# Cosine attention and token/channel mixing on one core: split score tiles, norms on ScalarE, permuted w2, squares further ahead

## Chip, cores and metric

The kernel runs on one core of one Trainium2 chip. The metric is device time in microseconds (us), median of several executions. The granted clock is the share of full speed that the profile shows. Kernels are compared only within the same rounds. The engines are PE (TensorE matmul), PEld (its weight load), DVE (VectorE), ACT (ScalarE), POOL (GpSimd) and SP (it issues most transfers). SBUF is the on-chip memory that holds the kernel's tiles, PSUM the one that its matmuls write to; copying a result from PSUM to SBUF is called its eviction.

## The reference

Cut to what matters:

```python
# q, k, v: (8, 12, 448, 64)
q_n = q / (norm(q, axis=-1) + 1e-6);  k_n = k / (norm(k, axis=-1) + 1e-6)
attn = softmax(q_n @ k_n.T / 0.1)
x = (attn @ v) -> (8, 448, 768)                        # heads side by side
u = x + (relu(x.T @ w_tok1) @ w_tok2).T                # token mixing, hidden size 256
out = u + relu(u @ w_ch1) @ w_ch2                      # channel mixing, hidden size 1536
```

## The kernel before

The work is 48 pairs of heads, six to a batch item. One loop iteration `i` does the scores of pair `i`, attn·v of pair `i-1` and the token step of about pair `i-2`; it also prepares later pairs (squares, sums, norms, scaling, transposes). Channel mixing of a batch item (`ch_units`) starts when its six pairs are done, so it cannot start before iteration 8, and from then on it is spread over the iterations by `feed`. A sequence position is split as `(p c)`, with `c` of size 4: row `4p+c` of the sequence sits in partition `p`, chunk `c`.

```python
    def squares(i, on_act=False):              # POOL, except in the prologue
        sq = nrm.tile([SC, 2, 2 * NCH, E], FP32, tag="sq", bufs=2)
        ...
                nc.gpsimd.tensor_mul(out=sq[:, a], in0=src, in1=src)
    def sums(i): nc.vector.tensor_reduce(out=ssq..., in_=sq, op=ALU.add)
    def rnorms(n, p0=0, p1=HP):                # 1/(sqrt(ssq) + eps)
        nc.scalar.activation(out=rn, in_=ssq, func=AF.Ln, bias=tiny[:])
        nc.scalar.activation(out=rn, in_=rn, func=AF.Exp, scale=0.5)
        nc.vector.tensor_scalar_add(out=rn, in0=rn, scalar1=EPS_NORM)
        nc.vector.reciprocal(out=rn, in_=rn)
    def scaled(i, dve=""): ...                 # qn, kn = q*rn, k*rn: POOL, or DVE where named

    def score(i, cg):                          # two chunks into one 4-bank PSUM tile, one exp
        psS = ps2.tile([128, 2, 2, 512], FP32, tag="s")          # ps2 has bufs=1
        ...
        nc.scalar.activation(out=st["pt"][:, cg], in_=psS[0:SC, :, :, 0:S], func=AF.Exp, scale=inv_tau)

    def m_tok2(i):                             # u = x + r @ w2, x added by four identity matmuls
        psU = ps.tile([128, S], FP32, tag="b")
        for tt in range(TT):
            nc.tensor.matmul(psU[:], st["r"][:, tt, :], w2t[:, tt, 0:S], start=(tt == 0), stop=False)
        for c in range(NCH):
            nc.tensor.matmul(psU[:].rearrange("d (p c) -> d c p", c=NCH)[:, c, :], st["x"][:, c, :],
                             id16[:, LEAD[c]:LEAD[c] + SC], start=False, stop=(c == NCH - 1))
        nc.vector.tensor_copy(out=ut[:, dt, 0:S], in_=psU[:])    # odd batch items: 384 and 64 columns
    ... # cut
    sq_at = at({p: p - 3 if p < 10 else max(p - 6, 2 + p // 2) for p in range(3, NP_ALL)})
    sc_at = at({p: p - 2 if p < DMA_FROM else p - 3 for p in range(2, NP_ALL)})
        # in iteration i, first: scaled(p) for p in sc_at[i], then squares(p) for p in sq_at[i]
        # at its end: sums(p), and for p < 15 rnorm1(p) at once
```

## Time and profile before

| | kernel before |
|---|---|
| time | 456.50 us median (456.25 to 456.67, 4 runs) |
| span of the profiled run | 455.0 us |
| busy | PE 408.4 (90%), DVE 202.8, ACT 236.8, POOL 213.5 us |

Shares over the whole span hide that there are two regimes. The table of busy time by stretch shows it. Its columns are the stretch and its length, then busy us and number of instructions of each engine, the granted clock, the DMA share and GB/s:

```profile
core 0: us, PE busy (x) PEld busy (x) DVE busy (x) ACT busy (x) POOL busy (x), PEclk, DMA share, GB/s
...
70.00:80.00 10.00, 1.89 (x15) 0.83 (x13) 8.55 (x7) 2.94 (x5) 9.98 (x11) 0.69 0.82 124
...
160.00:200.00 40.00, 39.77 (x414) 24.29 (x413) 19.71 (x49) 23.14 (x26) 25.82 (x25) 1.00 0.78 170
```

From 160 to 200 us PE is busy 99% of the time, so only PE work that disappears shortens that part. From 70 to 80 us PE does almost nothing and POOL is busy all the time. The clock column seems to miss a slow clock at the start: a group of four score matmuls takes 0.93 us at 56.89 us, where the column reads 0.50 (57 to 58 us), and 0.93 us at 21.28 us too, where it reads 1.00; later it takes 0.55 us.

In the PE-bound part, the chain of waits (start us, length us, what) gives the exact cost of each piece of PE work:

```profile
182.35 0.38 PE psU_2556 L257 x4
182.73 1.14 PE psG_0_2565 L269 x6
...
190.31 0.38 PE psU_2679 L257 x4
190.69 1.14 PE psG_4_2688 L269 x6
```

One iteration takes 190.69 - 182.73 = 7.96 us. The four identity matmuls of the token step (L257) take 0.38 us of it, 95 ns each.

In the early part the same chain goes round several engines:

```profile
60.94 1.14 DVE ssq_381 L155
62.10 0.32 ACT rn_382 L162
62.44 0.22 ACT rn_382 L163
62.69 0.18 DVE rn_382 L164
62.89 0.25 DVE rn_382 L165
...
64.29 1.04 POOL kn_817 L176
65.33 2.00 POOL sq_819 L150 x2
67.36 1.23 DVE ssq_381 L155
```

From one sum (L155) to the next is 67.36 - 60.94 = 6.42 us, and that is the length of an early iteration: the sum must wait for the squares, the squares stand behind the scaling in POOL's queue, and the scaling waits for the norm of the previous sum.

The standstill at 70 us, in the timeline (start, length, engine, line, operation):

```profile
70.14 1.48 POOL L135 CAST vt_95<-vs_380 112x1536 f16<-112x1536 f32 x1
...
71.36 6.27 DVE L164 TENSOR_SCALAR rn_382<-rn_382 112x16 f32<-112x16 f32 x1 [0.62 <-ACT rn_382 L163]
...
76.57 1.03 POOL L150 TENSOR_TENSOR sq_931<-kh_702 112x512 f32<-112x512 f32 x1
77.55 0.88 POOL L112 DMA_DIRECT2D wc2t<-in_moe_w_ch_dram  x1
...
78.56 0.53 PE L188 MATMUL pst_990<-id_83,kn_817 112*128 112x112 f16 x4 [8.11 <-DVE x_950 L225]
```

An add of 16 columns that takes 0.175 us elsewhere lasts 6.27 us while POOL runs one operation after another, and PE waits 8.11 us for DVE.

### The profile page before, as it was taken

The page shows a single profiled execution, that of the slowest core. Times are in us where ns is not written, and L with a number is a line of the kernel's source. Part 1 is how long each engine was busy: PE and PEld are TensorE (multiplying, and loading weights), DVE is VectorE, ACT ScalarE, POOL GpSimd, SP SyncE. Part 2 cuts the span into 40 slices and gives each one's busy share as a digit, 9 for nine tenths or more (in the row PEclk, how much of TensorE's full clock was granted, in tenths as well). Part 3 has the DMA queues.
Part 4 walks back from the last instruction along what each step waited for, and adds up shares of the span by engine and source line. Part 5 has one row for each costly group of instructions (what it writes and reads, how often), then busy time and mean ns, then how long its engine had stood idle before and what let it go on. Part 6 is the DMA issues. An engine that isn't in the chain of part 4 may idle for free.

```text
span 455.0 us, 9700 instructions
## 1 busy us (share of the span) xinstructions
PE 408.4 (90%) x4104; PEld 250.4 (55%) x4104; DVE 202.8 (45%) x458; ACT 236.8 (52%) x277; POOL 213.5 (47%) x216
## 2 busy tenths in 40 slices
PE   1377572899999999999999999999999999999995
PEld 0146451466655666556655666556656665566563
DVE  3656758565444354444534445446343433232000
ACT  3466543475466545675466455665565447630410
POOL 2686779391919265563838091926474330000000
PEclk9999987899999999999999999999999999999998
DMA  8999877752775169662685279733852233001012
GB/s 212 250 254 239 145 182 109 141 134 71 176 177 154 27 179 159 168 161 68 167 177 143 61 134 218 193 86 98 195 83 77 58 110 56 1 1 71 35 51 89
DMA packets 76411, 58.11 MB, mean 128 GB/s; under 512 B 36976, under 2 KB 72784, under 8 KB 76368
## 3 DMA queue, kind: packets, MB, share of 16 engines
q1 hardware_dynamic: 72704, 52.32, 48.0%
q0 software_dynamic: 3664, 5.18, 6.9%
q8 instruction: 32, 0.52, 0.5%
q14 instruction: 11, 0.09, 0.1%
HBM read 43.38 MB, written 11.01 MB: 120 GB/s over the span
## 4 chain that ended last, share of the span: by engine, by line
PE 80%; DVE 7%; ACT 6%; POOL 4%; issue 2%; DMA 1%; SPq 0%; ACTq 0%; POOLq 0%
DVE rn_382 L164 1%; DVE ssq_130 L155 1%; DVE ssq_381 L155 1%; DMA kh_104<-in_k_dram 1%; ACT pt_308 L210 1%; DVE ssq_118 L155 1%; DVE ssq_704 L155 0%; PE psG_2_1016 L269 0%; PE psF_1_0_3760 L288 0%; PE psF_1_0_2231 L288 0%; PE psF_0_0_2105 L288 0%; PE psF_2_1_1719 L288 0%; PE psF_1_0_5275 L288 0%; PE psF_1_1_1595 L288 0%; PE psF_0_1_1466 L288 0%
## 5 line engine op out<-in xcount | busy, mean ns | idle before, releaser
L269 PEld LDWEIGHTS <-wc1t 128*128 128x128 f16 x576 | 53.8, 101 | 45.1 <-issue 7.2
L233 PEld LDWEIGHTS <-w1t 128*128 128x128 f16 x384 | 22.7, 98 | 0.0
L288 PEld LDWEIGHTS <-gt_0_449 128*128 128x128 f16 x168 | 15.7, 98 | 10.9 <-issue 1.9
L288 PEld LDWEIGHTS <-gt_3_4834 128*128 128x128 f16 x168 | 15.9, 98 | 9.3
L288 PEld LDWEIGHTS <-gt_1_1784 128*128 128x128 f16 x168 | 15.8, 98 | 9.4 <-issue 0.4
L288 PEld LDWEIGHTS <-gt_2_3305 128*128 128x128 f16 x168 | 15.7, 98 | 9.5 <-issue 0.4
L188 PE MATMUL pst_156<-id_83,kn_154 112*128 112x112 f16 x4 | 0.6, 294 | 9.0 <-DVE kn_154 L176 9.0
L294 DVE COPY ost_0_6217<-psF_0_0_6218 128x384 f32<-128x384 f32 x1 | 0.6, 559 | 17.3 <-PE psF_0_0_6218 L291 17.3
L188 PE MATMUL pst_990<-id_83,kn_817 112*128 112x112 f16 x4 | 0.5, 286 | 8.1 <-DVE x_950 L225 8.1
L164 DVE TENSOR_SCALAR rn_382<-rn_382 112x16 f32<-112x16 f32 x3 | 6.6, 2206 | 1.9 <-ACT rn_382 L163 1.9
L176 POOL TENSOR_TENSOR qn_5263<-qh_4628,rn_4632 112x512 f16<-112x512 f32 x1 | 1.0, 1043 | 13.5 <-DVE rn_4632 L165 13.5
L176 POOL TENSOR_TENSOR qn_3745<-qh_3099,rn_3103 112x512 f16<-112x512 f32 x1 | 1.0, 1042 | 13.5 <-DVE rn_3103 L165 13.5
L176 POOL TENSOR_TENSOR qn_2216<-qh_1570,rn_1574 112x512 f16<-112x512 f32 x1 | 1.0, 1043 | 12.4 <-DVE rn_1574 L165 12.4
L176 POOL TENSOR_TENSOR qn_4510<-qh_3880,rn_3884 112x512 f16<-112x512 f32 x1 | 1.0, 1042 | 12.4 <-DVE rec_0_4542 L224 12.4
L176 POOL TENSOR_TENSOR qn_2981<-qh_2351,rn_2355 112x512 f16<-112x512 f32 x1 | 1.0, 1042 | 11.3 <-DVE rec_0_3013 L224 11.3
L176 POOL TENSOR_TENSOR qn_2611<-qh_1952,rn_1956 112x512 f16<-112x512 f32 x1 | 1.0, 1042 | 11.1 <-DVE rn_1956 L165 11.1
L176 POOL TENSOR_TENSOR qn_1839<-qh_1193,rn_1197 112x512 f16<-112x512 f32 x1 | 1.0, 1042 | 10.5 <-DVE rn_1197 L165 10.5
L176 POOL TENSOR_TENSOR qn_1452<-qh_808,rn_812 112x512 f16<-112x512 f32 x1 | 1.0, 1042 | 10.1 <-PE psO_0_1485 L221 10.1
L162 ACT ACTIVATE rn_107<-ssq_106,tiny 112x16 f32<-112x16 f32 x3 | 0.9, 307 | 9.1 <-DVE ssq_106 L155 9.1
L176 POOL TENSOR_TENSOR qn_4132<-qh_3481,rn_3485 112x512 f16<-112x512 f32 x1 | 1.0, 1044 | 9.6 <-DVE rn_3485 L165 9.6
L188 PEld LDWEIGHTS <-kn_154 112*128 112x128 f16 x4 | 0.3, 130 | 9.0 <-DVE kn_154 L176 9.0
L176 POOL TENSOR_TENSOR qn_4889<-qh_4246,rn_4250 112x512 f16<-112x512 f32 x1 | 1.0, 1042 | 9.0 <-DVE rn_4250 L165 9.0
(1681 smaller groups left out, 1266.8 us busy)
## 6 DMA issues: line engine op xcount, KB each, us to landing
wc1t<-in_moe_w_ch_dram POOLq DMA_DIRECT2D x2, 1152.0 KB, 10.9
wc2t<-in_moe_w_ch_dram POOLq DMA_DIRECT2D x2, 1152.0 KB, 9.5
qh_103<-in_q_dram SPq DMA_DIRECT2D x3, 224.0 KB, 4.3
kh_104<-in_k_dram SPq DMA_DIRECT2D x3, 224.0 KB, 4.6
vs_105<-in_v_dram SPq DMA_DIRECT2D x1, 672.0 KB, 7.0
qh_115<-in_q_dram SPq DMA_DIRECT2D x3, 224.0 KB, 8.1
kh_116<-in_k_dram SPq DMA_DIRECT2D x3, 224.0 KB, 8.3
vs_117<-in_v_dram SPq DMA_DIRECT2D x1, 672.0 KB, 10.7
```

The lines of the kernel that those rows point to most:

```text
L155: nc.vector.tensor_reduce(out=half[i // HP]["ssq"][:, :, lo:lo + 2 * NCH], in_=pipe[i]["sq"][:], axis=AXX.X, op=ALU.add)
L162: nc.scalar.activation(out=rn, in_=ssq, func=AF.Ln, bias=tiny[:])
L164: nc.vector.tensor_scalar_add(out=rn, in0=rn, scalar1=EPS_NORM)
L176: eng.tensor_tensor(out=dst[:].rearrange("p c g e -> p g c e"), in0=src, in1=_bcast_free(rn, E), op=ALU.mult)
L188: nc.tensor.transpose(pst[:, a, c, :], src[:, c], id16[:SC, :SC])
L210: nc.scalar.activation(out=st["pt"][:, cg], in_=psS[0:SC, :, :, 0:S], func=AF.Exp, scale=inv_tau)
L233: nc.tensor.matmul(psR[:, tt, :], w1t[:, m, tt * 128:(tt + 1) * 128], st["x"][:, m, :], start=(m == 0), stop=(m == NCH - 1))
L269: nc.tensor.matmul(psG[:], wc1t[:, dt, ct * 128:(ct + 1) * 128], ut[:, dt, span(b)], start=(dt == 0), stop=(dt == DT - 1))
L288: nc.tensor.matmul(psF[:], rows(gt, ct), wc2t[:, ct, dh * DH:(dh + 1) * DH], start=(ct == 0), stop=False)
L294: nc.vector.tensor_copy(out=o[:, 0:DH], in_=psF[:])
```

## The change

The intent: (1) take the add and the reciprocal of the norms from DVE, as two more ACT operations; (2) compute squares four pairs ahead (in the prologue and up to pair 11), with the norm one iteration after the sum, so that the loop over engines opens; (3) put the scores of one chunk in a 2-bank tile, two such tiles, one exp each; (4) place w2 in the order `(c p)` on chip, so that the identity matmuls write PSUM contiguously and the eviction undoes the order. Cut to its core:

```diff
-    ps2 = ctx.enter_context(tc.tile_pool(name="ps2", bufs=1, space=bass.MemoryType.PSUM))
+    ps2 = ctx.enter_context(tc.tile_pool(name="ps2", bufs=2, space=bass.MemoryType.PSUM))
+    def place_w2():
+        for tt in range(TT):
+            nc.gpsimd.tensor_copy(out=w2t[:, tt], in_=w2n[:, tt].rearrange("t (p c) -> t c p", c=NCH))
-        nc.vector.tensor_scalar_add(out=rn, in0=rn, scalar1=EPS_NORM)
-        nc.vector.reciprocal(out=rn, in_=rn)
+        nc.scalar.activation(out=rn, in_=rn, func=AF.Ln, bias=eps[:])
+        nc.scalar.activation(out=rn, in_=rn, func=AF.Exp, scale=-1.0)
-        psS = ps2.tile([128, 2, 2, 512], FP32, name=f"psS_{i}_{cg}", tag="s")
+        for c in range(c0, c1):
+            psS = ps2.tile([128, 2, 512], FP32, name=f"psS_{i}_{c}", tag="s")
+            ... # two matmuls
+            nc.scalar.activation(out=st["pt"][:, c], in_=psS[0:SC, :, 0:S], func=AF.Exp, scale=inv_tau)
-            nc.tensor.matmul(psU[:].rearrange("d (p c) -> d c p", c=NCH)[:, c, :], st["x"][:, c, :],
-                             id16[:, LEAD[c]:LEAD[c] + SC], start=False, stop=(c == NCH - 1))
+            nc.tensor.matmul(psU[:, c, :], st["x"][:, c, :], id16[:, LEAD[c]:LEAD[c] + SC],
+                             start=False, stop=(c == NCH - 1))
+        def rows(lo, n, p0, p1):
+            nc.vector.tensor_copy(out=ut[:, dt, lo:lo + n].rearrange("d (p c) -> d c p", c=NCH),
+                                  in_=psU[:, :, p0:p1])
-    sq_at = at({p: p - 3 if p < 10 else max(p - 6, 2 + p // 2) for p in range(3, NP_ALL)})
+    sq_at = at({p: p - 4 if p < 12 else max(p - 6, (p + 2) // 2) for p in range(4, NP_ALL)})
+    rn_at = at({p: p - 3 if p < 12 else (p + 4) // 2 for p in range(3, 15)})
-                scaled(p, dve="k" if p < 4 else "")
+            scaled(p, dve="k" if p < 7 else "")
-            if i == 0:
-                weights_tok()
+        if i == 1:
+            weights_tok()
+        if i == 2:
+            place_w2()
... # cut: order of loads and of the prologue, EARLY = 8 (below it, scores chunk by chunk)
```

More of the change, by code (lines that the diff above doesn't have):

```diff
@@ L81 @@
     nc.gpsimd.memset(tiny[:], 1e-18)
+    eps = cst.tile([SC, 1], FP32, name="eps")
+    nc.gpsimd.memset(eps[:], EPS_NORM)
     w1t = cst.tile([128, NCH, T], FP16, name="w1t")
-    w2t = cst.tile([128, TT, S + 384], FP16, name="w2t")
+    w2n = cst.tile([128, TT, S], FP16, name="w2n")
+    w2t = cst.tile([128, TT, NCH, SC], FP16, name="w2t")
     wc1t = cst.tile([128, DT, C], FP16, name="wc1t")
@@ L103, in weights_tok @@
         nc.gpsimd.dma_start(out=w1t[128 - SC:128, 3, :], in_=w1r[:, 3, :])
-        nc.gpsimd.dma_start(out=w2t[:, :, 0:S], in_=moe_w_tok2.rearrange("(tt p) s -> p tt s", p=128))
+        nc.gpsimd.dma_start(out=w2n[:], in_=moe_w_tok2.rearrange("(tt p) s -> p tt s", p=128))
+    def place_w2():
+        for tt in range(TT):
+            nc.gpsimd.tensor_copy(out=w2t[:, tt], in_=w2n[:, tt].rearrange("t (p c) -> t c p", c=NCH))
     def weights_ch1(i):
@@ L140, in sides, with squares @@
         return hf["q"][:, j:j + 2], hf["k"][:, j:j + 2]
-    def squares(i, on_act=False):
-        st = pipe[i] = {}
-        sq = nrm.tile([SC, 2, 2 * NCH, E], FP32, name=f"sq_{i}", tag="sq", bufs=2)
+    def squares(i, on_act=""):
+        if i not in pipe:
+            pipe[i] = {"sq": nrm.tile([SC, 2, 2 * NCH, E], FP32, name=f"sq_{i}", tag="sq", bufs=2)}
+        sq = pipe[i]["sq"]
         for a, src in enumerate(sides(i)):
             src = src.rearrange("p g c e -> p (g c) e")
-            if on_act:
+            if not on_act:
+                nc.gpsimd.tensor_mul(out=sq[:, a], in0=src, in1=src)
+            elif "qk"[a] in on_act:
                 nc.scalar.activation(out=sq[:, a], in_=src, func=AF.Square)
-            else:
-                nc.gpsimd.tensor_mul(out=sq[:, a], in0=src, in1=src)
-        st["sq"] = sq
     def sums(i):
@@ L188, in tpose, with qk_copy @@
                 nc.tensor.transpose(pst[:, a, c, :], src[:, c], id16[:SC, :SC])
-        nc.vector.tensor_copy(out=qk_tile(i)[:], in_=pst[:])
+        st["pst"] = pst
+    def qk_copy(i):
+        nc.vector.tensor_copy(out=qk_tile(i)[:], in_=pipe[i]["pst"][:])
     def dma_tpose(i):
@@ L195, in dma_tpose, with score @@
             nc.sync.dma_start_transpose(out=qk[:, a], in_=src[:].rearrange("p c g e -> p (c g e)"))
-    def score(i, cg):
+    def score(i, c0, c1):
         st = pipe[i]
         qk = st["qk"][:].rearrange("p a c s -> p (a c s)")
-        if cg == 0:
-            st["pt"] = ptp.tile([SC, 2, 2, 2, S], FP16, name=f"pt_{i}", tag="pt")
-        psS = ps2.tile([128, 2, 2, 512], FP32, name=f"psS_{i}_{cg}", tag="s")
-        for j in range(2):
-            c = 2 * cg + j
+        if c0 == 0:
+            st["pt"] = ptp.tile([SC, NCH, 2, S], FP16, name=f"pt_{i}", tag="pt")
+        for c in range(c0, c1):
+            psS = ps2.tile([128, 2, 512], FP32, name=f"psS_{i}_{c}", tag="s")
             for hh in range(2):
                 hb = hh * 64
-                nc.tensor.matmul(psS[:, hh, j, 0:S], qk[hb:hb + 64, c * SC:c * SC + 128],
+                nc.tensor.matmul(psS[:, hh, 0:S], qk[hb:hb + 64, c * SC:c * SC + 128],
                                  qk[hb:hb + 64, S:2 * S], start=True, stop=True)
-        nc.scalar.activation(out=st["pt"][:, cg], in_=psS[0:SC, :, :, 0:S], func=AF.Exp, scale=inv_tau)
+            nc.scalar.activation(out=st["pt"][:, c], in_=psS[0:SC, :, 0:S], func=AF.Exp, scale=inv_tau)
     def pv(i, hh):
@@ L220, in pv @@
             for c in range(NCH):
-                nc.tensor.matmul(psO[:, m, 0:E + 1], st["pt"][:, c // 2, hh, c % 2, lo:lo + 128],
+                nc.tensor.matmul(psO[:, m, 0:E + 1], st["pt"][:, c, hh, lo:lo + 128],
                                  vt[:, g, c, 0:E + 1], start=(c == 0), stop=(c == NCH - 1))
@@ L251, in m_tok2 @@
         ut = pairt[b // 2][0]
-        psU = ps.tile([128, S], FP32, name=f"psU_{i}", tag="b")
+        psU = ps.tile([128, NCH, SC], FP32, name=f"psU_{i}", tag="b")
         for tt in range(TT):
-            nc.tensor.matmul(psU[:], st["r"][:, tt, :], w2t[:, tt, 0:S],
-                             start=(tt == 0), stop=False)
+            nc.tensor.matmul(psU[:], st["r"][:, tt, :], w2t[:, tt], start=(tt == 0), stop=False)
         for c in range(NCH):
-            nc.tensor.matmul(psU[:].rearrange("d (p c) -> d c p", c=NCH)[:, c, :], st["x"][:, c, :],
-                             id16[:, LEAD[c]:LEAD[c] + SC], start=False, stop=(c == NCH - 1))
+            nc.tensor.matmul(psU[:, c, :], st["x"][:, c, :], id16[:, LEAD[c]:LEAD[c] + SC],
[3 more added lines that the diff above has]
+                                  in_=psU[:, :, p0:p1])
         if b % 2 == 0:
-            nc.vector.tensor_copy(out=ut[:, dt, 0:S], in_=psU[:])
+            rows(0, S, 0, SC)
         else:
-            nc.vector.tensor_copy(out=ut[:, dt, S + 64:2 * S], in_=psU[:, 0:384])
-            nc.vector.tensor_copy(out=ut[:, dt, S:S + 64], in_=psU[:, 384:S])
+            rows(S + 64, 384, 0, 96)
+            rows(S, 64, 96, SC)
     def m_ch1(b, ct):
@@ L330, in at, with gpsimd_part @@
         return got
-    load_at = at({p: p - 6 if p < 13 else max(p - 8, (p - 1) // 2) for p in range(9, NP_ALL)})
-    sq_at = at({p: p - 3 if p < 10 else max(p - 6, 2 + p // 2) for p in range(3, NP_ALL)})
+    load_at = at({p: p - 6 if p < 13 else max(p - 8, 6) for p in range(9, NP_ALL)})
+    sq_at = at({p: p - 4 if p < 12 else max(p - 6, (p + 2) // 2) for p in range(4, NP_ALL)})
+    rn_at = at({p: p - 3 if p < 12 else (p + 4) // 2 for p in range(3, 15)})
     sc_at = at({p: p - 2 if p < DMA_FROM else p - 3 for p in range(2, NP_ALL)})
     tok_at = at({p: max(p + 2, 3 if p < 1 else 4) for p in range(NP_ALL)})
+    EARLY = 8
+    def gpsimd_part(i):
+        for p in sc_at.get(i, ()):
+            scaled(p, dve="k" if p < 7 else "")
+        for p in sq_at.get(i, ()):
+            squares(p)
+        if i == 1:
+            weights_tok()
+        if i == 2:
+            place_w2()
+        if i in (2, 4):
+            weights_ch1(i // 4)
+        if i in (6, 8):
+            weights_ch2((i - 6) // 2)
+        if i and (i + 2) % HP == 0 and 1 <= (i + 2) // HP < NHALF:
+            cast_v((i + 2) // HP)
     with tc.manual_schedule():
-        load_qk(0)
-        load_qk(1)
+        for p in range(3):
+            load_qk(p)
         load_v(0)
-        for p in range(2, 5):
+        for p in range(3, 5):
             load_qk(p)
@@ L346 @@
             load_qk(p)
-        squares(0, on_act=True)
+        squares(0, on_act="qk")
         sums(0)
+        squares(1, on_act="q")
         rnorm1(0)
-        squares(1, on_act=True)
+        squares(1, on_act="k")
         squares(2)
@@ L353 @@
         tpose(0)
-        cast_v(0)
         sums(1)
+        qk_copy(0)
         rnorm1(1)
-        scaled(1, dve="qk")
+        scaled(1, dve="q")
         sums(2)
-        rnorm1(2)
+        squares(3)
         for i in range(NP_ALL + 2):
+            if DMA_FROM <= i + 2 < NP_ALL:
+                dma_tpose(i + 2)
             for p in load_at.get(i, ()):
@@ L364 @@
                 load_v((i + 4) // HP)
-            if DMA_FROM <= i + 2 < NP_ALL:
-                dma_tpose(i + 2)
-            for p in sc_at.get(i, ()):
-                scaled(p, dve="k" if p < 4 else "")
-            for p in sq_at.get(i, ()):
-                squares(p)
-            if i == 0:
-                weights_tok()
-            if i in (2, 4):
-                weights_ch1(i // 4)
-            if i in (7, 8):
-                weights_ch2(i - 7)
-            if (i + 2) % HP == 0 and 1 <= (i + 2) // HP < NHALF:
-                cast_v((i + 2) // HP)
+            if i:
+                gpsimd_part(i)
             left = 6 - (i - 2) % NPAIR
             quota = max(sum(t for t, _ in queue) - 2000.0, 0.0) / left
-            if i < NP_ALL:
-                score(i, 0)
+            if i < EARLY:
+                score(i, 0, 1)
+                score(i, 1, 2)
+            elif i < NP_ALL:
+                score(i, 0, 2)
+            if i == 0:
+                cast_v(0)
+                rnorm1(2)
+                gpsimd_part(0)
+                sums(3)
+            for p in rn_at.get(i, ()):
+                rnorm1(p)
             feed(quota * 0.25)
@@ L388 @@
                 m_tok1(p)
+            if i < EARLY:
+                score(i, 2, 3)
             feed(quota * 0.25, 400.0)
@@ L391 @@
                 tpose(i + 1)
-            if i < NP_ALL:
-                score(i, 1)
+                qk_copy(i + 1)
+            if i < EARLY:
+                score(i, 3, 4)
+            elif i < NP_ALL:
+                score(i, 2, 4)
             for p in tok_at.get(i, ()):
@@ L403 @@
                 sums(p)
-                if p < 15:
-                    rnorm1(p)
-                elif p % HP == HP - 1:
+                if p >= 15 and p % HP == HP - 1:
                     rnorms(p // HP)
```

## The prediction

> **What bounds the kernel now.** Two regimes. From about 85 us on, the table of busy time by stretch shows PE at 99 to 100% while ACT and DVE are near 55 and 45%: a steady iteration is PE work (chain of waits: 7.96 us from 182.73 to 190.69). Before that PE is not the limit: it is busy about 42 of the first 80 us, part of that on a slow clock (a 448-column score group of four takes 0.93 us at first, 0.55 us later). Scores of iterations 1 to 8 start 6.4 us apart (timeline: 21.3, 27.2, 33.2, 39.3, 46.2, 52.6, 60.2, 66.6). The chain there is a loop over engines: POOL squares 2.0, DVE sum 1.2, ACT Ln/Exp 0.55, DVE add and reciprocal 0.45, POOL scaling 2.1 us, then the next squares. At 71.36 us one DVE add of 112x16 takes 6.27 us instead of 0.175 while POOL runs back to back; PE stands still about 8 us and restarts slow. That add is SBUF to SBUF; the Trainium skill (SBUF — State Buffer, Who interferes with whom) says that such an op in a 2-port mode blocks against GpSimd. The trace agrees with a block.
>
> **What the change does.**
> 1. Norms on ACT: the add and the reciprocal leave DVE, two ACT ops of 0.2 to 0.3 us come. The 6.3 us block goes, with the slow restart: about 9 to 10 us, on the critical path.
> 2. Squares four pairs ahead: breaks the loop. Then ACT is the limit of an early iteration: four exps of 112x896 (estimate from 1.65 us for 1792: about 0.9 each, 3.6) plus norms 1.1 = 4.8 us; DVE comes to 4.7. With in-order bubbles I expect 5.4 us instead of 6.4 over seven iterations: about 7 us. The first iteration gains 1 us. Iteration 8 should start near 58 us, not 66.6.
> 3. Two score tiles: let PE fill one while ACT reads the other; it is what makes 5.4 us possible. In the steady part it is worth nothing, since PE does not wait for exp there. ACT gains 0.3 us an iteration, off the path.
> 4. w2 permuted: the four identity matmuls of the token step write PSUM with a step of four elements: 0.38 us for four (95 ns each) in the chain, against about 50 ns each for the transposes of equal width. The skill (PSUM — Partial Sum Buffer, Specifications) says non-contiguous patterns slow matmuls. Saves 0.18 us a pair, 41 pairs after 85 us: about 7.5 us, all PE-bound. DVE's copy (0.62 us) now scatters instead; I expect about the same length, off the path.
> 5. Given back: POOL is packed around iterations 5 to 8 (three squares and a cast in iteration 7, about 10 us of work); in-order sums on DVE then delay evictions: 3 us. The k scaling stays on DVE to pair 6 and reads two SBUF tensors, so it can still be blocked by POOL (one such took 1.60 instead of 0.69 us).
>
> Sum: 9.5 + 8 + 7.5 - 3, less some overlap in the cold early part: about 24 us less.
>
> **Predicted: 432 us**, 80% range 423 to 441. Faster by over 2%: 0.97; within 2%: 0.02; slower: 0.01.
>
> **What would show it.** Identity matmuls 45 to 55 ns apart; no DVE op over 2 us; score starts 5.0 to 5.8 us apart in iterations 1 to 7; iteration 8 near 58 us; steady iteration 7.78 us; ACT busy up by about 20 us; DVE eviction still about 0.6 us.
>
> **What would make it wrong.** The scattered eviction much slower; POOL waiting for the w2 transfer before placing it (9.3 us to landing now) and stalling squares; POOL's bunching around iteration 7 giving a new stall; DVE scaling starved by POOL as the add was; ACT's in-order queue delaying exps behind norms.

## The result

| | before | after |
|---|---|---|
| time | 456.50 us (456.25 to 456.67, 4 runs) | 437.73 us (436.53 to 439.43, 4 runs) |
| ratio of fast runs | | 0.9592, 95% interval 0.9558 to 0.9627 |
| span of the profiled run | 455.0 us | 436.3 us |
| busy PE / DVE / ACT / POOL | 408.4 / 202.8 / 236.8 / 213.5 us | 401.3 / 213.0 / 251.7 / 214.6 us |

A ratio here is the mean time of one kernel's fast runs over that of the kernel before in the same rounds, so it is not quite the ratio of the medians quoted. The gain is 18.8 us in the medians. The forecast was 432 us, a gain of some 24 us: the time lies in the range, the gain is 5 to 6 us short. (The terms of the prediction's sum, 9.5 + 8 + 7.5 - 3, make 22 us and not 24, before the overlap that it meant to take off. So 2 us or more of what is missing are a slip in the sum.)

The same stretches of the kernel after, in the table of busy time by stretch (columns as above):

```profile
70.00:80.00 10.00, 10.00 (x94) 5.45 (x91) 5.26 (x11) 7.24 (x15) 9.98 (x11) 0.84 0.64 104
...
160.00:200.00 40.00, 39.31 (x425) 23.29 (x423) 20.31 (x42) 26.40 (x44) 19.18 (x20) 1.00 0.64 146
```

The chain of waits in the PE-bound part:

```profile
167.49 0.20 PE psU L265 x4
167.69 1.13 PE psG L282 x6
...
175.27 0.20 PE psU L265 x4
175.46 0.57 PE psG L282 x3
```

The iteration is 175.46 - 167.69 = 7.77 us; the identity matmuls (now L265) take 0.20 us for four. This step is as forecast.

Where PE first does the scores of iteration i, and the transposes that end iteration 8, from the timelines of the profiled runs (us; the runs below the second row are the experiments that follow):

| run | i=1 | 2 | 3 | 4 | 5 | 6 | 7 | 8 | transposes for 9 | 9 |
|---|---|---|---|---|---|---|---|---|---|---|
| before | 21.3 | 27.2 | 33.2 | 39.3 | 46.2 | 52.6 | 60.2 | 66.6 | 78.6 | 85.7 |
| after | 20.1 | 25.2 | 31.8 | 39.1 | 49.5 | 53.8 | 58.3 | 62.7 | 69.2 | 75.2 |
| norms_alone | 22.5 | 28.6 | 35.1 | 41.3 | 48.1 | 56.1 | 63.1 | 69.6 | 73.8 | 81.7 |
| squares_near | 17.0 | 25.4 | 33.5 | 41.1 | 48.0 | 56.8 | 64.1 | 71.7 | 75.6 | 81.4 |
| w2_late | 19.8 | 24.9 | 32.8 | 38.5 | 51.4 | 56.2 | 60.7 | 65.2 | 71.6 | 76.1 |
| kpool_w2late | 19.5 | 24.9 | 29.1 | 40.7 | 47.3 | 52.2 | 56.7 | 61.2 | 67.6 | 73.7 |
| squares_spread | 19.8 | 24.9 | 31.5 | 39.2 | 48.6 | 53.5 | 58.0 | 62.5 | 66.8 | 71.2 |
| all_four | 19.1 | 24.5 | 29.6 | 40.4 | 45.8 | 49.8 | 54.3 | 58.5 | 62.7 | 67.1 |

After the change, iterations 5 to 7 take 4.3 to 4.5 us, shorter than the 5.4 I forecast. But iterations 2 to 4 take 6.6, 7.3 and 10.4 us, and there is a new standstill in iteration 8. From the transposes for iteration 9 to the end the kernel before needs 455.0 - 78.6 = 376.4 us and the kernel after 436.3 - 69.2 = 367.1 us. So about half of the gain lies on each side of that point.

Two places of the timeline after show where the early part loses. First, iteration 4:

```profile
36.22 1.09 POOL L111 COPY w2t<-w2n 128x448 f16<-128x448 f16 x2 [4.65 <-PE pst L195]
...
42.18 1.03 POOL L156 TENSOR_TENSOR sq<-qh 112x512 f32<-112x512 f32 x1
42.38 3.05 DVE L183 TENSOR_TENSOR kn<-kh,rn 112x512 f16<-112x512 f32 x1
...
44.16 0.88 POOL L115 DMA_DIRECT2D wc1t<-in_moe_w_ch_dram  x1
...
46.38 0.93 PE L263 MATMUL psU<-w2t,r 128*128 128x448 f16 x2 [4.15 <-DVE r L245]
```

POOL stood still 4.65 us before it placed w2 (the profile names PE as releaser; the w2 transfer, issued at 25.9 us and 10.3 us to landing, is the likelier one). Then DVE's k scaling, 0.68 us when alone, lasted 3.05 us beside POOL's stream, and PE waited 4.15 us for DVE. Second, iteration 8:

```profile
65.17 1.04 POOL L156 TENSOR_TENSOR sq<-qh 112x512 f32<-112x512 f32 x1 [1.39 <-DVE ssq L162]
67.25 1.22 DVE L162 TENSOR_REDUCE ssq<-sq 112x16 f32<-112x1024 f32 x1 [1.03 <-POOL sq L156]
69.16 0.36 PE L195 MATMUL pst<-id,kn 112*128 112x112 f16 x4 [2.01 <-DVE x L234]
```

Iteration 7 has the squares of three pairs. The third pair waits for a buffer (a sum on DVE), DVE then waits for these squares, and PE waits for what stands behind them in DVE's queue.

Third, the eviction of psU (groups by line, shapes kept apart: busy us, mean ns of one, idle before):

```profile
L269 DVE CAST ut<-psU 128x448 f16<-128x448 f32 x24 | 28.0, 1167 | 41.8 <-PE psU L265 41.8
```

1167 ns instead of the 624 ns before (L260 there). I had forecast no change.

### The profile page after: what moved, and what is told of

It reads as the page before. It is cut to its first block, busy times and chain, and to the rows that moved or that the text cites. A ratio compares the mean times of both kernels' runs of the same rounds, so it can differ in the third digit from the quotient of the medians.

```text
span 436.3 us, 9810 instructions
## 1 busy us (share of the span) xinstructions
PE 401.3 (92%) x4104; PEld 241.0 (55%) x4104; DVE 213.0 (49%) x408; ACT 251.7 (58%) x425; POOL 214.6 (49%) x217
## 4 chain that ended last, share of the span: by engine, by line
PE 79%; POOL 6%; DVE 4%; ACT 4%; DMA 3%; issue 2%; SPq 0%; POOLq 0%; DVEq 0%; ACTq 0%
PE psF L301 24%; PE psG L282 24%; PE psO L230 9%; PE psS L217 8%; PE psU L263 5%; PE psR L242 4%; POOL sq L156 3%; ACT pt L219 2%; PE psF L304 2%; DMA w1t<-in_moe_w_tok_dram 2%; PE psU L265 2%; DVE ssq L162 2%; DMA qh<-in_q_dram 1%; DVE kn L183 1%; POOL qn L183 1%
## 5 line engine op out<-in xcount | busy, mean ns | idle before, releaser
L219 ACT ACTIVATE pt<-psS 112x896 f16<-112x896 f32 x192 | 164.7, 915 | 38.8 <-PE psS L217 38.7
L282 PE MATMUL psG<-ut,wc1t 128*128 128x448 f16 x576 | 122.8, 354 | 0.2 <-ACT gt L284 0.2
L301 PE MATMUL psF<-wc2t,gt 128*128 128x384 f16 x672 | 118.4, 326 | 0.0
L269 DVE CAST ut<-psU 128x384 f16<-128x384 f32 (+1 forms) x72 | 55.9, 842 | 86.9 <-PE psU L265 86.9
L301 PEld LDWEIGHTS <-gt 128*128 128x128 f16 x672 | 62.8, 98 | 38.5 <-issue 2.1
L284 ACT ACTIVATE gt<-psG 128x448 f16<-128x448 f32 x96 | 51.6, 545 | 52.8 <-PE psG L282 50.9
L217 PE MATMUL psS<-qk 64*128 64x448 f16 x384 | 58.5, 367 | 12.4 <-ACT pt L219 8.0
L230 PEld LDWEIGHTS <-pt 112*128 112x128 f16 x1536 | 59.9, 99 | 15.5 <-issue 8.8
L230 PE MATMUL psO<-vt,pt 112*128 112x65 f16 x1536 | 66.7, 196 | 0.0
L162 DVE TENSOR_REDUCE ssq<-sq 112x16 f32<-112x1024 f32 x48 | 58.0, 1210 | 10.0 <-POOL sq L156 5.0
L309 ACT COPY ost<-psF 128x384 f32<-128x384 f32 x28 | 13.4, 478 | 56.8 <-PE psF L304 56.8
L307 DVE COPY ost<-psF 128x384 f32<-128x384 f32 x28 | 15.6, 558 | 56.8 <-PE psF L304 47.5
## 6 DMA issues: line engine op xcount, KB each, us to landing
wc2t<-in_moe_w_ch_dram POOLq DMA_DIRECT2D x2, 1152.0 KB, 10.8
```

Source lines behind the costliest of these rows:

```text
L162: nc.vector.tensor_reduce(out=half[i // HP]["ssq"][:, :, lo:lo + 2 * NCH], in_=pipe[i]["sq"][:], axis=AXX.X, op=ALU.add)
L217: nc.tensor.matmul(psS[:, hh, 0:S], qk[hb:hb + 64, c * SC:c * SC + 128], qk[hb:hb + 64, S:2 * S], start=True, stop=True)
L219: nc.scalar.activation(out=st["pt"][:, c], in_=psS[0:SC, :, 0:S], func=AF.Exp, scale=inv_tau)
L230: nc.tensor.matmul(psO[:, m, 0:E + 1], st["pt"][:, c, hh, lo:lo + 128], vt[:, g, c, 0:E + 1], start=(c == 0), stop=(c == NCH - 1))
L269: nc.vector.tensor_copy(out=ut[:, dt, lo:lo + n].rearrange("d (p c) -> d c p", c=NCH), in_=psU[:, :, p0:p1])
L282: nc.tensor.matmul(psG[:], wc1t[:, dt, ct * 128:(ct + 1) * 128], ut[:, dt, span(b)], start=(dt == 0), stop=(dt == DT - 1))
```

## The experiments

Twelve kernels ran, all with correct results, in five rounds each. My theory: the steady half is the identity matmuls; the early half is squares ahead plus norms off DVE; the shortfall is waits on POOL and DVE in iterations 2 to 8. The rivals: the longer eviction is the shortfall; or the two score tiles make the early gain; or the order of loads does.

| kernel | median us (range) | ratio to before (95% interval) |
|---|---|---|
| after (the change) | 437.73 (436.53 to 439.43) | 0.9592 (0.9558 to 0.9627) |
| w2_alone | 449.76 (448.90 to 450.75) | 0.9853 (0.9829 to 0.9878) |
| norms_alone | 453.90 (452.55 to 454.84) | 0.9940 (0.9913 to 0.9967) |
| one_exp | 438.93 (437.95 to 439.86) | 0.9615 (0.9591 to 0.9638) |
| copy_in_order | 436.24 (435.19 to 436.65) | 0.9553 (0.9530 to 0.9576) |
| squares_near | 446.18 (445.22 to 446.99) | 0.9779 (0.9750 to 0.9808) |
| squares_spread | 434.72 (434.26 to 436.27) | 0.9536 (0.9507 to 0.9565) |
| w2_late | 439.77 (439.08 to 440.82) | 0.9644 (0.9615 to 0.9673) |
| k_on_pool | 437.12 (435.52 to 438.57) | 0.9582 (0.9551 to 0.9612) |
| kpool_w2late | 436.45 (433.84 to 436.92) | 0.9530 (0.9497 to 0.9562) |
| spread_copy | 433.68 (433.09 to 434.60) | 0.9484 (0.9456 to 0.9512) |
| all_four | 431.03 (430.17 to 432.12) | 0.9429 (0.9398 to 0.9461) |
| cast_on_act | 431.33 (429.91 to 432.74) | 0.9431 (0.9401 to 0.9461) |

The experiments were run in three batches, on three different chips, each beside the kernel before, whose medians were 456.33, 456.61 and 456.65 us. So I compare ratios, and call a difference of less than about 2 us shown only where the trace shows it too.

### One part alone: w2_alone

To the kernel before, only the permuted w2:

```diff
-    w2t = cst.tile([128, TT, S + 384], FP16, name="w2t")
+    w2n = ...; w2t = cst.tile([128, TT, NCH, SC], FP16, name="w2t")
+            if i == 2:
+                place_w2()
     # and m_tok2 as in the change
```

> The kernel before with only the permuted w2 (placed on chip in iteration 2) and the token step that goes with it. Theory (contiguous PSUM writes are the gain of the steady part): identity matmuls at 50 ns instead of 95 ns, steady iteration near 7.78 us instead of 7.96, 7 to 8.5 us less after the first 85 us; the longer DVE eviction (1.16 us) costs at most 1 us early. So 448 to 450 us, ratio 0.982 to 0.986. Rival (the scattered eviction costs PE time, and the steady gain comes from elsewhere): above 453 us.

Measured: 449.76 us, 6.6 us less than before, at the edge of what the theory expected. The identity matmuls' records have a median of 213 ns against 301 ns before, as in the kernel after, and the early part is unchanged (iteration 8 at 66.9 us against 66.6). So this part is worth 6.6 us, all of it in the PE-bound part, and the longer eviction does not cancel it.

### One part alone: norms_alone

To the kernel before, only the two ACT operations in place of DVE's add and reciprocal:

```diff
-        nc.vector.tensor_scalar_add(out=rn, in0=rn, scalar1=EPS_NORM)
-        nc.vector.reciprocal(out=rn, in_=rn)
+        nc.scalar.activation(out=rn, in_=rn, func=AF.Ln, bias=eps[:])
+        nc.scalar.activation(out=rn, in_=rn, func=AF.Exp, scale=-1.0)
```

> The kernel before with only the norms' add and reciprocal moved from DVE to ACT. Theory: the 6.27 us block of the add and the standstill of PE at 70 to 78 us vanish: 447 to 451 us. Rival (the standstill only changes its cause, since GpSimd is packed in iterations 7 and 8, and DVE then waits for the squares in order): PE still idle for several us near 70 us, 453 to 457 us.

Measured: 453.90 us, only 2.4 us less. Neither text has it right: the time lies in the rival's range, but not for the rival's reason. The standstill does vanish; the timeline at the place where the kernel before waits 8.11 us:

```profile
73.78 0.36 PE L190 MATMUL pst<-id,kn 112*128 112x112 f16 x4 [0.26 <-DVE x L227]
```

From score 8 to these transposes it is 73.8 - 69.6 = 4.2 us instead of 12.0, which is the 8 us I counted. But iteration 8 itself starts 3.1 us later than before (69.6 against 66.6). The exps of a pair stand behind four norm operations in ACT's queue instead of two. The timeline of one iteration, of the kernel before and then of norms_alone:

```profile
48.11 0.31 ACT L162 ACTIVATE rn_131<-ssq_130,tiny 112x16 f32<-112x16 f32 x1 [2.30 <-DVE ssq_130 L155]
48.57 1.65 ACT L210 ACTIVATE pt_612<-psS_0_613 112x1792 f16<-112x1792 f32 x1
50.27 0.55 PE L208 MATMUL psS_1_662<-qk_553 64*128 64x448 f16 x4 [2.08 <-ACT pt_612 L210]
```

```profile
50.04 0.31 ACT L164 ACTIVATE rn<-ssq,tiny 112x16 f32<-112x16 f32 x1 [2.30 <-DVE ssq L157]
51.09 1.65 ACT L212 ACTIVATE pt<-psS 112x1792 f16<-112x1792 f32 x1
52.79 0.93 PE L210 MATMUL psS<-qk 64*128 64x448 f16 x4 [2.66 <-ACT pt L212]
```

The exp starts 1.05 us after the first norm operation instead of 0.46, and PE waits 2.66 us for it instead of 2.08. Not all of the 3.1 us is this: 1.2 us are there at iteration 1 already, about half of them because a k scaling beside POOL's cast took 1.94 us, so that the next sum began at 15.85 us instead of 15.20. By the transposes 7.8 - 3.1 = 4.7 us are gained; from there to the end norms_alone takes 452.2 - 73.8 = 378.4 us and the kernel before 376.4, so 2.0 us are lost again (from 120 to 360 us PE is busy 237.1 us instead of 238.6). What is left is 2.7 us, about the 2.8 us between the two profiled spans.

### One part undone: squares_near

The changed kernel with the squares where the kernel before has them:

```diff
-    sq_at = at({p: p - 4 if p < 12 else max(p - 6, (p + 2) // 2) for p in range(4, NP_ALL)})
-    rn_at = at({...})
+    sq_at = at({p: p - 3 if p < 10 else max(p - 6, 2 + p // 2) for p in range(3, NP_ALL)})
+    rn_at = {}                 # and rnorm1(p) straight after sums(p), for p < 15
-        squares(3)             # and no sums(3) in iteration 0
```

> The changed kernel with the squares where the kernel before has them (three pairs ahead, the norm straight after the sum); two score tiles, ACT norms and permuted w2 as changed. Theory: the loop over GpSimd, DVE and ACT returns, score starts 6.2 to 6.6 us apart in iterations 1 to 8, iteration 8 at 66 to 69 us, and 445 to 449 us: squares ahead are the largest part of the early gain. Rival (the gain of the early part comes from the order of loads and DMA, not the squares): 438 to 441 us.

Measured: 446.18 us; score starts are 6.9 to 8.8 us apart, and iteration 8 starts at 71.7 us. The ratio differs from the change's by 0.0187, which is 8.5 us of 456.5. So squares ahead and the norm an iteration after its sum, which this run undoes together, are the largest part of the gain. The chain of waits of this run shows what holds it now:

```profile
41.97 1.17 DVE ssq L162
43.17 0.32 ACT rn L169
...
44.31 0.81 ACT pt L219
45.16 0.36 PE psS L217 x2
...
47.05 2.18 DVE ut L269 x2
...
49.72 1.14 DVE ssq L162
```

From sum to sum it is 7.75 us, and from 33.9 to 74.9 us the chain has no POOL operation at all. It is the second road of the kernel before, made longer by two norm operations in front of the exps and by the longer eviction (1.17 instead of 0.62 us, see below). In the change the norm comes an iteration after its sum and behind the first two exps, and the squares are further ahead, so both roads can open. Which of the two edits is worth how much was not run. The order of loads, which this run keeps, cannot be the 8.5 us; what it is worth by itself was not run either.

### One part undone: one_exp

The changed kernel with one 4-bank score tile and one exp for two chunks in all iterations:

```diff
-    ps2 = ctx.enter_context(tc.tile_pool(name="ps2", bufs=2, space=bass.MemoryType.PSUM))
+    ps2 = ctx.enter_context(tc.tile_pool(name="ps2", bufs=1, space=bass.MemoryType.PSUM))
-            psS = ps2.tile([128, 2, 512], FP32, name=f"psS_{i}_{c}", tag="s")
+        psS = ps2.tile([128, 2, 2, 512], FP32, name=f"psS_{i}_{cg}", tag="s")
     # and one exp after the four matmuls, as in the kernel before
-    EARLY = 8
+    EARLY = 0
```

> The changed kernel with one 4-bank score tile and one exp for two chunks, as in the kernel before; all else as changed. Theory (the two tiles let PE fill one while ACT reads the other, only of use in iterations 0 to 7): early iterations go from 4.5 us to about 5.5 us, 442 to 446 us. Rival (early iterations are bound by GpSimd and DVE, so two tiles are worth nothing): 437 to 439 us. ACT busy falls by about 8 us.

Measured: 438.93 us; the ratio is 0.0023 (1 us) above the change's, with overlapping intervals. In the trace, iterations 5 to 7 take 4.9 to 5.4 us instead of 4.3 to 4.5, yet that is lost again at the standstill of iteration 8 (iteration 9 starts at 75.0 us, in the kernel after at 75.2). So the rival is closer: two tiles are worth about 1 us here, which is not clear of the noise. What they are worth where the standstill is gone, as in squares_spread, was not run. The Trainium skill ("ScalarE: Activation LUTs", What ACT_TABLE_LOAD costs) says that back-to-back activations overlap by about 93 ns, so that splitting one is cheap. The trace agrees: one exp of 896 columns takes 0.92 us, two take 1.72 us together in the timeline (0.12 us less than twice 0.92), and one of 1792 takes 1.65.

### The eviction: copy_in_order

```diff
-            nc.vector.tensor_copy(out=ut[:, dt, lo:lo + n].rearrange("d (p c) -> d c p", c=NCH),
-                                  in_=psU[:, :, p0:p1])
+            nc.vector.tensor_copy(out=ut[:, dt, lo:lo + n].rearrange("d (p c) -> d p c", c=NCH),
+                                  in_=psU[:, :, p0:p1].rearrange("d c p -> d p c"))
```

> The changed kernel, but the eviction of psU writes SBUF in order and reads PSUM with the step. If the step of the SBUF write makes it 1.16 us, it returns to 0.62 us; if any step does, it stays. Theory that the eviction is off the critical path after 70 us and costs 0.5 us in each of few early iterations: 435 to 438 us. Rival (DVE bounds the early part, the longer eviction is the missing 6 us of my prediction): 432 us or less.

The group by line of this run, to be held against that of the kernel after:

```profile
L269 DVE CAST ut<-psU 128x448 f16<-128x448 f32 x24 | 15.0, 624 | 42.3 <-PE psU L265 42.3
```

Measured: 436.24 us. It is the step of the 2-byte SBUF write (8 bytes from one element to the next) that made the eviction longer; reading PSUM with a step costs DVE nothing. The ratio falls by 0.0039 (1.8 us), with intervals that overlap slightly, so the rival that the eviction is the whole shortfall falls.

### The waits of the early part: squares_spread

```diff
+    sq_at[7].remove(13); sq_at[8].insert(0, 13)
+    rn_at[8].remove(13); rn_at[9].insert(0, 13)
```

> The changed kernel with the squares of pair 13 in iteration 8 instead of 7 (its norm in 9). Theory: iteration 7 has three squares on GpSimd, and the third's sum, in order on DVE, holds up evictions: PE is idle 2.4 us near 67 us and slow until 73 us. Spread: no wait there, iteration 9 starts 3 to 4 us earlier, 433.5 to 436 us. Rival (the wait moves one iteration on, where PE is already bound): 437 to 439 us.

Measured: 434.72 us, every run below every run of the change. The transposes for 9 start at 66.8 us and not 69.2, and iteration 9 at 71.2 and not 75.2: PE no longer waits there and does not run slow afterwards. The Trainium skill ("TensorE: Matmul & The Clock Gate", Part 1) says that the clock of PE halves after an idle window of about 3.4 us. The trace agrees on the halving, but not on the length. In the kernel after PE stood still only 2.01 us before the transposes at 69.16 us, and then the granted clock was 0.50; six channel matmuls took 2.08 us there. In this run, where there is no wait, the clock stayed at 1.00 and they take 1.30 us. The stretch of the kernel after, then of this run:

```profile
70.00:72.00 2.00, 2.00 (x12) 0.87 (x9) 0.56 (x2) 2.00 (x4) 2.00 (x3) 0.50 0.00 2
```

```profile
70.00:72.00 2.00, 2.00 (x25) 0.89 (x22) 1.78 (x4) 0.89 (x3) 1.98 (x3) 1.00 0.01 2
```

The length of one wait does not decide alone: in the kernel before, 2.30 us at 56.89 us were followed by a clock of 0.50, and 2.08 us at 50.27 us were not.

### The waits of the early part: w2_late, k_on_pool, and both (kpool_w2late)

```diff
 # w2_late
-        if i == 2:
+        if i == 3:
             place_w2()
 # k_on_pool
-            scaled(p, dve="k" if p < 7 else "")
+            scaled(p)
```

> The changed kernel, but w2 is placed in iteration 3, not 2. Theory: GpSimd's 4.65 us wait for the w2 transfer holds up the squares, through them DVE's sums and the k scaling, and makes iteration 4 10.4 us long. Without it scores of iteration 5 start 3 to 5 us earlier (44.5 to 46.5 instead of 49.5) and the kernel takes 433 to 435 us. Rival (GpSimd catches up, as it is four pairs ahead, and the gap has another cause): 437 to 438 us.

> The changed kernel with the k scaling of pairs 2 to 6 on GpSimd instead of DVE. Theory that DVE's scaling starves while GpSimd runs back to back (3.71, 3.05 and 1.37 us for 0.69): DVE loses all operations over 2.4 us, and the early part gets 1 to 3 us shorter although GpSimd has 1.04 us more per iteration: 434.5 to 437 us. Rival (GpSimd's own length binds early): 439 us or more.

w2_late took 439.77 us, about 2 us more than the change, which neither theory expected. Its timeline says why:

```profile
40.74 6.50 DVE L183 TENSOR_TENSOR kn<-kh,rn 112x512 f16<-112x512 f32 x1
...
41.23 1.48 POOL L142 CAST vt<-vs 112x1536 f16<-112x1536 f32 x1
...
45.65 1.03 POOL L156 TENSOR_TENSOR sq<-kh 112x512 f32<-112x512 f32 x1
...
48.17 0.93 PE L263 MATMUL psU<-w2t,r 128*128 128x448 f16 x2 [6.57 <-DVE r L245]
```

POOL's wait for w2 fell to 1.5 us, so its stream became denser, and DVE's two-input scaling, which reads SBUF beside it, was held for 6.50 us, through a cast, two scalings and two squares; it ended 0.56 us after the last of these. So the wait that I meant to remove was probably one of the gaps in which DVE got through (argued from this timeline).

k_on_pool took 437.12 us, the same as the change. DVE loses these holds, as expected. But POOL, now without a pause from 17.4 us on except for 4.62 us of waiting for the w2 transfer, takes over the delay. If each remedy uncovers what the other removes, the two together should help:

> The changed kernel with both of two edits that bought 0.6 us and nothing on their own: k scaling of pairs 2 to 6 on GpSimd, and w2 placed in iteration 3. Theory (each hides the other: with k on DVE, GpSimd's wait for w2 is the gap in which DVE's blocked scaling gets through; with k on GpSimd its stream has that one wait of 4.62 us left and no other): score of iteration 8 near 58 to 60 us instead of 62.4 to 65.2, 432 to 435 us. Rival (neither matters, something else bounds the early part): 437 us or more.

Measured: 436.45 us. The ratio is 0.0062 (2.8 us) below the change's, but the intervals touch and the median is above what I expected, so this is a partial miss. Iteration 8 starts at 61.2 us, not at 58 to 60. What is left is a wait that the other two had covered, on PE:

```profile
34.65 1.14 PE L242 MATMUL psR<-x,w1t 128*128 128x128 f16 x8 [3.74 <-DMA w1t<-in_moe_w_tok_dram]
```

In the chain of waits of the change itself this transfer is already the longest piece of the early part (8.71 us from 25.34 us on), though PE waits only 0.23 us for it there. Here PE waits for w1. The change issues the token weights in iteration 1 (w1 at 24.6 us), where the kernel before issues them in iteration 0 (at 21.1 us), and PE now wants them sooner. The transfers take 8.0 us to land before and 8.8 to 9.1 us here.

### Together: spread_copy, all_four, cast_on_act

spread_copy has squares_spread and copy_in_order; all_four adds w2_late and k_on_pool; cast_on_act is all_four with

```diff
+        if n in (1, 2, 3): nc.scalar.copy(out=dst, in_=src)
+        else: nc.gpsimd.tensor_copy(out=dst, in_=src)
```

> The changed kernel with pair 13's squares one iteration later and the eviction of psU written in order. If the two gains (2.5 and 1.5 us) are of different waits they add: 432.5 to 434.5 us. If the shorter eviction only fed the same wait on iteration 7's squares: 434 to 436 us.

> k scaling on GpSimd, w2 placed in iteration 3, pair 13's squares in iteration 8, eviction in order. Theory that GpSimd's uninterrupted stream is then the bound of iterations 1 to 8: 429 to 432 us, GpSimd over 95% busy from 20 to 70 us. Rival (gains overlap): 433 us or more.

> As all_four, with the v casts of halves 1 to 3 (1.48 us each on GpSimd, in iterations 1, 4 and 7) on ACT. Theory that GpSimd's length bounds the early part: 2 to 4 us less than all_four, 426 to 430 us. Rival (ACT, 4.5 us an iteration, is the bound by then): the same as all_four or 1 to 3 us more.

spread_copy: 433.68 us, so the two gains add, as expected for different waits. all_four: 431.03 us, 5.7% under the kernel before and about 1.7% under the change; it beats both kernels. Iteration 8 starts at 58.5 us, about where I had forecast it for the change itself.

But the theory I attached to all_four, that POOL's stream is the bound, gets no support from cast_on_act. POOL is 99.5% busy from 20 to 70 us in all_four (49.76 of 50 us), as I expected. The tables by stretch of all_four and then of cast_on_act:

```profile
40.00:60.00 20.00, 18.94 (x277) 12.54 (x275) 17.31 (x38) 17.77 (x34) 19.80 (x21) 0.96 1.14 244
```

```profile
40.00:60.00 20.00, 18.44 (x270) 12.77 (x268) 16.16 (x35) 17.49 (x33) 17.77 (x19) 0.92 1.14 243
```

In cast_on_act POOL has 2 us less to do in this stretch, and the time is the same: 431.33 us. An engine that is 99% busy because work was queued for it early is not thereby the limit. The run is no clean test, since the casts now load ACT. In all_four, iteration 3 is 10.7 us long, and in it PE waits for w1 (3.5 us in the waits; 3.5 us in those of cast_on_act too); iterations 5 to 7 take 4.0 to 4.4 us. That is near the 4.4 us of ACT in one early iteration (3.32 for four exps and 1.1 for four norm operations, by the timeline after). That ACT is the bound there is argued from these numbers, not tested.

Open, for want of runs: issuing w1 and w2 earlier. By the wait in all_four it could be worth up to 3.5 us (an estimate).

## Why the prediction was right, and where it was not

- **Range and direction: right.** 437.7 us lies in 423 to 441, and faster by over 2% was given 0.97.
- **"w2 permuted ... about 7.5 us, all PE-bound": right.** 0.38 to 0.20 us for four matmuls, a steady iteration of 7.77 us for the 7.78 forecast, and 6.6 us for this part alone. That reading came from setting the strided matmuls beside transposes of equal width in the same trace, and from the Trainium skill ("PSUM — Partial Sum Buffer", Specifications), which says that non-contiguous patterns slow matmuls.
- **"Squares four pairs ahead: breaks the loop", 7 us and 1 us for the first iteration: right as a sum.** Undone, together with the later norm, it costs 8.5 us. The loop over POOL was only one of two roads: with the squares near, the chain runs over the norm, the exps behind it and the eviction, and not over POOL, so "breaks the loop" is not shown for the distance of the squares by itself. Its detail was wrong twice: iterations 5 to 7 take 4.3 to 4.5 us and not 5.4, and iterations 2 to 4 take 6.6 to 10.4, because of the holds on DVE and the token weights. I had named the holds and the wait for w2 under what would make the prediction wrong, and gave them no number.
- **"Norms on ACT: ... about 9 to 10 us, on the critical path": this is the step that failed.** The mechanism is as said, for the standstill of 8 us disappears in norms_alone. The mis-sized term is the net worth: 2.4 us. I counted the standstill and left out of the sum that the exps then stand behind twice as many norm operations in ACT's queue, though I had named this under what would make the prediction wrong: in the iteration shown an exp starts 0.59 us later, which over the iterations makes most of the 3.1 us by iteration 8 (argued from the timelines), and 2.0 us more are lost after the transposes. 2.4 us is the worth in the kernel before; the change with the norms put back on DVE was not run.
- **"Given back: POOL is packed around iterations 5 to 8 ... 3 us": right, and near in size.** Spreading the squares returns 2.6 us by the ratios.
- **"Two score tiles: ... what makes 5.4 us possible": not supported.** With one tile iterations 5 to 7 take 4.9 to 5.4 us, and about 1 us is lost, within the noise.
- **"DVE's copy ... about the same length": wrong.** 0.62 became 1.17 us. It is nearly off the path: about 2 us.
- **"ACT busy up by about 20 us": short.** It rose by 14.9 us.

The sum, as measured: norms 2.4 (alone), squares 8.5 (undone), w2 6.6 (alone), tiles about 1 (undone) make 18.5 us of the 18.8. That they add so well is partly luck, since alone and undone are not the same measure. The 8.5 us is also net of what is given back. Held against the prediction's terms, the norms came 7 us short (2.4 for 9.5) and the squares 3.5 us over (8.5 for 8 - 3). That the time lay in the range rests in part on these errors cancelling, which is luck.

## What to carry to other kernels

A standstill that a change removes is worth its length only if what replaces the cause is not in a queue in front of the critical work: cost the removed wait and the added queue time together, iteration by iteration. When removing one wait makes the kernel no faster or even slower, look for the engine that used that gap; two remedies that do nothing alone may each be hidden by the other, and the next wait is then worth looking for too. Where a strided access is moved from one operand to another, put it on the side where the trace shows it free: here PSUM reads by DVE, not PSUM writes by PE and not 2-byte SBUF writes by DVE.

## What the Trainium skill lacked or had wrong

- "SBUF — State Buffer", Who interferes with whom, says that whichever engine issues first gets the shared port pair for the whole instruction, and the other blocks. What it lacks is that the blocked DVE instruction need not get in after the POOL instruction in flight: it was held over many POOL instructions in a row (6.27 us for an add of 0.175 us, released as POOL issued a transfer; 6.50 us for a scaling of 0.68 us, until POOL fell idle). In other cases it got in after one (1.37 us). The runs do not show what decides.
- The cacheline note of the same page (under Door 1: The DMA port swizzle) says that 2-byte elements may be 8 apart for free. A DVE eviction from PSUM to SBUF that wrote fp16 with a step of 4 elements took 1167 ns for 448 columns; the same eviction written in order took 624 ns.
- "PSUM — Partial Sum Buffer", Specifications, says that non-contiguous patterns slow matmuls, without a size. Here a write step of 4 fp32 elements made a 112-column matmul 95 ns instead of 50 ns. The page does not say how DVE fares: reading PSUM with a step of 112 fp32 elements cost nothing (624 ns both ways).
- No page gives the landing time of small weight transfers issued by POOL while the input loads keep DMA full: 8.0 to 10.8 us for w1 and w2 in these runs, which decides how many iterations ahead they must be issued.
- "TensorE: Matmul & The Clock Gate", Part 1: the idle window cited under squares_spread is longer than the wait after which the clock was halved here, 2.01 us (granted clock 0.50).
